# Linear attention and a feed-forward layer: queries spread evenly ahead of the wide stage, gathered in float32, half of the normalising on ScalarE

## The chip, the cores and the metric

The kernel runs on one core of a Trainium2 chip. The metric is the device time of one execution in microseconds. An execution's time is a little longer than its span in the trace, which runs from the first to the last instruction.

## What is computed

The reference is linear attention with random features, and a feed-forward layer on its result. For each of 8 batches and 8 heads (576 tokens, head dimension 64, 128 features):

```python
def phi(x):
    proj = np.einsum('bhsd,md->bhsm', x, omega)
    sq = np.sum(x * x, axis=-1, keepdims=True) / 2.0
    h = proj - sq
    h = h - np.max(h, axis=-1, keepdims=True)
    return np.exp(h) / np.sqrt(m)
q_p, k_p = (phi(q_s), phi(k_s))
kv = np.einsum('bhsm,bhsd->bhmd', k_p, v)
z = np.sum(k_p, axis=2)
num = np.einsum('bhsm,bhmd->bhsd', q_p, kv)
den = np.einsum('bhsm,bhm->bhs', q_p, z)[..., None] + 1e-06
attn_out = num / den
x = attn_out.transpose(0, 2, 1, 3).reshape(B * S, H * D)   # 4608 x 512
h = x @ w_in                                                # 512 x 2048
g = h - np.tanh(h)
out = g @ w_out                                             # 2048 x 512
```

## The kernel before

The 4608 tokens are cut into 18 chunks of 256. A pair of heads (128 rows) is called c and runs from 0 to 3, so x of a chunk has four pieces. Nearly all products are made in a one-pass float format from an operand split in two: the rounded part and the rest (`xh` and `xl` for x, `gh` and `gl` for g, `qh` and `ql` for the queries' features).

Three stages follow each other on TensorE:

- Chunks 0 and 1, taken together as tiles 512 wide, while the weights are decoded (to about 173 us).
- Chunks 2 to 5 singly, 256 wide. `ffn_h` makes the tiles h of a chunk, two blocks of the 2048 at a time (s from 0 to 7), and `ffn_out` their products with w_out.
- Chunks 6 to 17 in six pairs of 512 tokens, the wide stage. `wide_h` makes one h tile 512 wide per block f (0 to 15) and its g; `wide_out` and the "last" products follow. h has two PSUM banks, so block f=2 waits until f=0's bank has been read by the tanh and by the subtraction g = h - tanh(h).

Attention runs beside this, in generators. A key unit (b, c) makes kv and z of a batch and a pair of heads. A query unit (ch, c), `q_unit`, makes one piece of x: it loads q (`qf`, by a DMA that SP issues), splits it (`qx`), makes the features (`pj`, then the exponential in `phi`), multiplies them by z to get the denominator (`dn`, line 350), takes the reciprocal and scales its four feature tiles by it (lines 354 to 359), transposes them (`pt`, line 366), splits them (`qh`, line 384, and `ql`, line 385), multiplies by kv (`pn`, lines 391 and 392) and gathers the result in `later` (lines 396 to 399: two copies on ScalarE, two additions on VectorE). From chunk 3 on pt and pn share one PSUM bank, and so do the units after each other. `x_split` (lines 407 and 408) then makes `xh` on ScalarE and `xl` on VectorE.

Both `later` and `xh`/`xl` hold two chunks, at ch % 2. Before the change a unit of chunks 3 to 5 calls `x_split` itself right after its gather (line 402), into the place that chunk ch - 2 was read from; for pairs from 6 on `next_x` splits both chunks at once when all their units are done.

What goes first is set in two steps. Tables of numbers give the beat at which each unit's generator is started (`start`, lines 643 to 655); the main program calls `beat()` twice per s or f, and each beat advances every open generator by one step. `tick((), True)` advances them without work of the main program, where a chunk is needed and its units aren't done. The instructions so recorded are then put in order by a scheduler, engine by engine. Each engine executes its list strictly in that order.

The engine that scales a tile is taken in rotation from a list (`norm`); from chunk 3 on this list reads:

```python
norm=[nc.vector, nc.vector, nc.vector, nc.scalar]
```

## Time and profile before

| | us |
|---|---|
| median of 3 runs | 1074.54 |
| lowest and highest | 1073.91, 1076.31 |
| the profiled execution's own time | 1075.36 |
| its span in the trace | 1073.6 |
| TensorE busy | 1041.5 (97%) |
| VectorE busy | 854.3 (80%) |
| ScalarE busy | 695.0 (65%) |
| GpSimd busy | 440.9 (41%) |

PE is TensorE's matmuls, DVE is VectorE, ACT is ScalarE, POOL is GpSimd, SP issues DMAs. The shares are means over stages: VectorE's falls after 900 us, when the last queries are done. Where an instruction waited, its row ends with the idle time of its engine in brackets and with the instruction that ended it. The granted clock is a share of TensorE's 2.4 GHz; it has two levels, 1.2 and 2.4 GHz, so a value between is a mean over a stretch.

### The profile page before, as it was taken

The page shows a single profiled execution, that of the slowest core. Times are in us where ns is not written, and L with a number is a line of the kernel's source. Part 1 is how long each engine was busy: PE and PEld are TensorE (multiplying, and loading weights), DVE is VectorE, ACT ScalarE, POOL GpSimd, SP SyncE. Part 2 cuts the span into 40 slices and gives each one's busy share as a digit, 9 for nine tenths or more (in the row PEclk, how much of TensorE's full clock was granted, in tenths as well). Part 3 has the DMA queues.
Part 4 walks back from the last instruction along what each step waited for, and adds up shares of the span by engine and source line. Part 5 has one row for each costly group of instructions (what it writes and reads, how often), then busy time and mean ns, then how long its engine had stood idle before and what let it go on. Part 6 is the DMA issues. An engine that isn't in the chain of part 4 may idle for free.

```text
span 1073.6 us, 19114 instructions
## 1 busy us (share of the span) xinstructions
PE 1041.5 (97%) x5608; PEld 889.1 (83%) x5608; DVE 854.3 (80%) x3006; ACT 695.0 (65%) x1809; POOL 440.9 (41%) x745
## 2 busy tenths in 40 slices
PE   8988999999999899899999999999999999999998
PEld 7766888999988898688888888888887888888886
DVE  5999995999999989989989888899889958742220
ACT  5997655777777778677767676677666746532220
POOL 3634540544543322556545563656355402221320
PEclk8999999999999999899999999999999999999999
DMA  8952722111211101222234332443243314332301
GB/s 261 295 172 90 283 96 70 33 34 53 55 53 33 53 16 57 72 77 78 78 109 137 103 118 88 130 138 117 65 142 115 104 45 146 114 101 82 104 1 39
DMA packets 85960, 106.18 MB, mean 99 GB/s; under 512 B 17632, under 2 KB 67936, under 8 KB 83808
## 3 DMA queue, kind: packets, MB, share of 16 engines
q1 hardware_dynamic: 85776, 104.92, 31.1%
q8 instruction: 45, 0.74, 0.3%
q14 instruction: 59, 0.48, 0.1%
q10 hardware_dynamic: 80, 0.03, 0.0%
HBM read 87.10 MB, written 17.83 MB: 98 GB/s over the span
## 4 chain that ended last, share of the span: by engine, by line
PE 67%; DVE 22%; issue 5%; ACT 4%; POOL 1%; DMA 0%; DVEq 0%; POOLq 0%; ACTq 0%
PE h_w L532 19%; PE h L471 7%; PE last L545 4%; PE last L547 4%; PE last L546 4%; DVE junk L350 3%; PE po_w L547 3%; PE po_w L546 3%; PE po_w L545 3%; PE po L489 2%; PE po L490 2%; PE po L491 2%; PE pk L269 2%; PE pt L366 2%; DVE phi_q L359 2%
## 5 line engine op out<-in xcount | busy, mean ns | idle before, releaser
L532 PE MATMUL h_w<-xh,w 128*128 128x512 f32 x768 | 253.9, 394 | 2.7 <-DVE g_w L536 2.6
L532 PEld LDWEIGHTS h_w<-xh,w 128*128 128x128 f32 x768 | 144.1, 189 | 31.1 <-DVE g_w L536 4.2
L532 PE MATMUL h_w<-xl,w 128*128 128x512 f32 x384 | 151.3, 394 | 0.9 <-DVE xl L408 0.9
L471 PE MATMUL h<-xh,w 128*128 128x256 f32 (+1 forms) x640 | 147.2, 307 | 3.8 <-DVE g L476 2.2
L540 POOL CAST w<-g_w 128x256 fp32r<-128x256 f32 x96 | 41.0, 427 | 224.2 <-DVE g_w L536 208.5
L471 PEld LDWEIGHTS h<-xh,w 128*128 128x128 f32 x640 | 107.5, 190 | 11.8 <-DVE g L476 3.1
L350 DVE CUSTOM_DVE_ANT_0 junk<-phi_q,zb 128x128 f32<-128x128 f32 (+1 forms) x320 | 105.3, 331 | 13.1 <-ACT phi_q L153 1.0
L536 DVE TENSOR_TENSOR g_w<-h_w,g_w 128x512 f32<-128x512 f32 x96 | 66.0, 687 | 60.6 <-ACT g_w L535 59.9
L471 PE MATMUL h<-xl,w 128*128 128x256 f32 (+1 forms) x320 | 97.5, 305 | 2.1 <-DVE xl L408 2.1
L153 ACT ACTIVATE phi_q<-phi_q,nb_q 128x128 f32<-128x128 f32 x240 | 82.5, 394 | 19.6 <-DVE nb_q L149 18.7
L535 ACT ACTIVATE g_w<-h_w 128x512 f32<-128x512 f32 x96 | 56.8, 591 | 57.1 <-PE h_w L532 53.4
L253 POOL TENSOR_TENSOR khl<-phi_ka,khl 128x256 fp32r<-128x256 f32 x48 | 38.3, 798 | 127.3 <-DVE khl L252 105.5
L532 PEld LDWEIGHTS h_w<-xl,w 128*128 128x128 f32 x384 | 72.8, 190 | 14.4 <-DVE xl L408 1.3
L541 POOL TENSOR_TENSOR w<-g_w,w 128x256 fp32r<-128x256 f32 x96 | 80.0, 833 | 4.6
L440 POOL TENSOR_SCALAR a<-a 128x1024 f32<-128x1024 f32 x14 | 59.0, 4213 | 54.4 <-ACT a L436 36.0
L545 PE MATMUL po_w<-w,ge_w 128*128 128x512 f32 x192 | 75.9, 395 | 0.0
L545 PE MATMUL last<-w 128*128 128x512 f32 x192 | 75.4, 393 | 0.0
L546 PE MATMUL po_w<-w,ge_w 128*128 128x512 f32 x192 | 75.3, 392 | 0.0
L547 PE MATMUL last<-w 128*128 128x512 f32 x192 | 75.2, 392 | 0.0
L546 PE MATMUL last<-w 128*128 128x512 f32 x192 | 75.1, 391 | 0.0
L537 ACT CAST ge_w<-g_w 128x256 fp32r<-128x256 f32 x96 | 39.1, 407 | 55.6 <-DVE g_w L536 53.9
L547 PE MATMUL po_w<-w,ge_w 128*128 128x512 f32 x192 | 72.2, 395 | 1.3 <-DVE ge_w L538 1.2
(173 smaller groups left out, 2911.9 us busy)
## 6 DMA issues: line engine op xcount, KB each, us to landing
w<-w_in SPq DMA_DIRECT2D x320, 128.0 KB, 2.4
raw<-w SPq DMA_DIRECT2D x16, 1024.0 KB, 8.1
kf<-kT SPq DMA_DIRECT2D x32, 288.0 KB, 3.2
qf<-qT SPq DMA_DIRECT2D x72, 128.0 KB, 2.2
out<-o SPq DMA_DIRECT2D x36, 256.0 KB, 2.1
w_in<-w SPq DMA_DIRECT2D x16, 512.0 KB, 3.4
v<-vt SPq DMA_DIRECT2D x24, 288.0 KB, 2.9
v<-va SPq DMA_DIRECT2D x8, 288.0 KB, 5.9
```

The lines of the kernel that those rows point to most:

```text
L153: nc.scalar.activation(ph[:, j], ph[:, j], AF.Exp, bias=nb[:, j : j + 1], scale=-1.0)
L350: nc.vector.tensor_tensor_reduce(bank("junk")[r], ph[r, i], kvs[b, c][1][r, h], scale=1.0, scalar=EPS, op0=ALU.mult, op1=ALU.add, accum_ou ...
L440: engine.tensor_scalar(a.bitcast(F32), a.bitcast(F32), 2.0**-15, 122879.9921875, op0=ALU.max, op1=ALU.min)
L471: nc.tensor.matmul(o, w_, x, start=i == 0, stop=i == len(prods) - 1)
L532: nc.tensor.matmul(p, w_, x, start=i == 0, stop=i == len(prods) - 1)
L535: nc.scalar.activation(g, p, AF.Tanh)
L536: nc.vector.tensor_sub(g, p, g)
L540: nc.gpsimd.tensor_copy(hi, g[:, 1])
L541: nc.gpsimd.tensor_sub(lo, g[:, 1], hi.bitcast(F32))
L545: nc.tensor.matmul(o, h, wt[f][:, 0, DM:], start=f == 0, stop=False)
L546: nc.tensor.matmul(o, h, wt[f][:, 1, DM:], start=False, stop=False)
L547: nc.tensor.matmul(o, l, wt[f][:, 0, DM:], start=False, stop=f == NF - 1)
```

## The change

A query unit of chunks 3 to 5 no longer splits its x. It gathers x in float32 in `later`, once the chunk that holds the place (ch - 2) has been split (the set `split`). The main program splits a chunk: `x_of(ch)` makes the four pieces' `xh` and `xl`, at the chunk's start if it hasn't been done, or ahead of that, in the chunk before, if all four units have been recorded by then. Chunks 6 and 7 are split in the same way during chunk 5 where they can be; later pairs as before. The tables of starts are new for the queries of chunks 3 to 9 and the keys of batches 2 to 4. The rotation of the scaling is `[nc.vector, nc.scalar]`, so two of four tiles go to each engine.

```diff
--- before.py
+++ after.py
@@ -390,16 +390,13 @@
                 w = kvs[b, c][0][:, h * P : (h + 1) * P]
                 nc.tensor.matmul(pn[:, h, s:e], w, qh[:, h, s:e], start=True, stop=False)
                 nc.tensor.matmul(pn[:, h, s:e], w, ql[:, h, s:e], start=False, stop=True)
-        while ch >= C0 and gathered < (ch - C0) // 2:
+        while ch > 3 and ch - 2 not in split:
             yield
         xs = later[:, c, ch % 2 * TC : ch % 2 * TC + TC]
         nc.scalar.copy(xs[0:D], pn[D:P, 0])
         nc.scalar.copy(xs[D:P], pn[0:D, 1])
         nc.vector.tensor_add(xs[0:D], pn[0:D, 0], xs[0:D])
         nc.vector.tensor_add(xs[D:P], pn[D:P, 1], xs[D:P])
-        if ch < C0:
-            yield
-            x_split(ch, c, xs, nc.vector)
         xdone[ch] = xdone.get(ch, 0) + 1
 
     def x_split(ch, c, x, engine):
@@ -556,7 +553,7 @@
 
     need = {b: (b * S) // TC for b in range(B)}
     xdone = {}
-    gathered = 0
+    split = {2}
     gens = []
 
     def tick(new=(), force=False):
@@ -627,7 +624,7 @@
     kvf.clear()
     ak = open_pool("ak")
     mode.update(
-        chain=False, native=False, norm=[nc.vector, nc.vector, nc.vector, nc.scalar], junk=[junk],
+        chain=False, native=False, norm=[nc.vector, nc.scalar], junk=[junk],
         hi=nc.scalar, pj=["pj0"], pk=["pk"], pt=["pj0"],
         phi=(ak, 3), qh=(ak, 1), ql=(ak, 1), kf=(ak, 1), kx=(ak, 1), qf=(ak, 1),
         qx=(ak, 1), vr=(ak, 1), khl=(ak, 2), vhl=(ak, 2), zs=(ak, 1), c1=(ak, 1), kvs=(ak, 1))
@@ -644,14 +641,14 @@
         a, j = (ch - C0) // 2, (ch - C0) % 2 * NC
         for c in range(NC):
             if ch < C0 + 2:
-                k = [(28,32,36,40),(41,45,49,53),(56,60,63,66),(58,68,72,75),(78,81,83,85)][ch - 3][c]
+                k = [(28,31,34,37),(43,46,49,52),(40,55,58,63),(61,66,69,72),(75,78,80,83)][ch - 3][c]
             else:
-                k = begins(a - 1) + -9 + 10 * (j + c) // 2
+                k = begins(a - 1) + (-4 + 9 * (j + c) // 2 if a == 1 else -9 + 5 * (j + c))
             start.setdefault(k, []).append(("q", ch, c))
     for b in range(2, B):
         a = ((b * S) // TC - C0) // 2
         for c in range(NC):
-            k = [31,51][b - 2] + [5,5][b - 2] * c if b < 2 + len([31,51]) else begins(a - 1) + -18 + 11 * c
+            k = [28,48,82][b - 2] + [5,5,9][b - 2] * c if b < 2 + len([28,48,82]) else begins(a - 1) + -18 + 11 * c
             start.setdefault(k, []).append(("k", b, c))
     t = 32 - 2 * (NF - done)
     assert min(start) >= t and all(k == int(k) for k in start)
@@ -669,12 +666,24 @@
     ffn_store(0)
     mode.update(pj=["pj0", "pj1"], pt=["pt"])
     prev = None
+
+    def x_of(ch):
+        split.add(ch)
+        for c in range(NC):
+            x_split(ch, c, later[:, c, ch % 2 * TC : ch % 2 * TC + TC], nc.vector)
+
     for ch in range(2, C0):
         out_tiles(ch)
+        while xdone[ch] < NC:
+            tick((), True)
+        if ch not in split:
+            x_of(ch)
         for s in range(NS):
-            while ch > 2 and xdone.get(ch, 0) < NC:
-                tick((), True)
+            if s > 0 and ch + 1 not in split and xdone.get(ch + 1) == NC:
+                x_of(ch + 1)
             g = (ch, s, *ffn_h(ch, s))
+            if ch == C0 - 1 and s == NS - 1 and xdone.get(C0 + 1) == NC:
+                x_of(C0 + 1)
             beat()
             if prev is not None:
                 ffn_out(*prev)
@@ -690,13 +699,17 @@
     mode.update(o=["g", "gl"])
 
     def next_x(a):
-        nonlocal gathered
-        for ch in (C0 + 2 * a, C0 + 2 * a + 1):
+        pair = (C0 + 2 * a, C0 + 2 * a + 1)
+        for ch in pair:
             while xdone.get(ch, 0) < NC:
                 tick((), True)
-        gathered = a + 1
-        for c in range(NC):
-            x_split(slice(0, 2), c, later[:, c].rearrange("p (j t) -> p j t", j=2), nc.vector)
+        if split.isdisjoint(pair):
+            for c in range(NC):
+                x_split(slice(0, 2), c, later[:, c].rearrange("p (j t) -> p j t", j=2), nc.vector)
+            split.update(pair)
+        for ch in pair:
+            if ch not in split:
+                x_of(ch)
 
     next_x(0)
     for a in range(NL):
```

What the new tables and the new place of the split do to the order stands in the programs. The names carry chunk and c: `qf_5_0` is the load of unit (5,0), `pt_7_3` the transposes of unit (7,3), `ka4_1`, `km4_1` and `kb4_1` the parts of key unit (4,1); `h_4_0` is the h tile of chunk 4, s=0, `h_w0_1` that of the first wide pair, f=1.

SP, the loads of queries, keys (`kf`) and values (`v`) from the one of (4,0) on, before:

```order
L84 DMA qf_4_0_2331<-qT 128x256
L84 DMA kf_2_3_2691<-kT 128x576
L84 DMA qf_4_1_2624<-qT 128x256
L235 DMA v_2_2_2335<-vt 128x576
L84 DMA qf_4_2_2895<-qT 128x256
L84 DMA kf_3_0_3029<-kT 128x576
L502 DMA out<-o_640_2867 128x512
L235 DMA v_2_3_2693<-vt 128x576
L502 DMA out<-o_512_2864 128x512
L84 DMA qf_4_3_3141<-qT 128x256
L84 DMA qf_5_0_3334<-qT 128x256
```

With the change, the same place:

```order
L84 DMA qf_5_0_2414<-qT 128x256
L84 DMA kf_2_3_2591<-kT 128x576
L235 DMA v_2_2_2256<-vt 128x576
L84 DMA qf_4_0_2589<-qT 128x256
L84 DMA qf_4_1_2821<-qT 128x256
L84 DMA kf_3_0_2948<-kT 128x576
L499 DMA out<-o_640_2967 128x512
L235 DMA v_2_3_2593<-vt 128x576
L499 DMA out<-o_512_2964 128x512
L84 DMA qf_4_2_3008<-qT 128x256
L84 DMA qf_4_3_3226<-qT 128x256
```

The load of unit (5,0), which stood behind all of chunk 4, now stands ahead of (4,0).

TensorE, where chunk 4 begins. Before, the last products of unit (4,3) and the first of chunk 4:

```order
L392 MATMUL pn_4_3_3512<-ql_4_3_3437,kvw_2_3_3235 128x128
L391 MATMUL pn_4_3_3512<-qh_4_3_3436,kvw_1_3_996 128x128
L145 MATMUL pj_ka3_1_2_3478<-om_89,kx_3_1_3377 128x256 x2
L392 MATMUL pn_4_3_3512<-ql_4_3_3437,kvw_1_3_996 128x128
L391 MATMUL pn_4_3_3512<-qh_4_3_3436,kvw_2_3_3235 128x128
L392 MATMUL pn_4_3_3512<-ql_4_3_3437,kvw_2_3_3235 128x128
L489 MATMUL po1_3_2780<-w13_1523,gh_3_6_3571 128x512
L490 MATMUL po1_3_2780<-w13_1523,gh_3_6_3571 128x512
L491 MATMUL po1_3_2780<-w13_1523,gl_3_6_3572 128x512
L471 MATMUL h_4_0_3832<-xh_100,w0_220 128x256
```

With the change, from the transposes of unit (4,3) on:

```order
L366 MATMUL pt_4_3_3503<-ident_64,phi_q4_3_3320 128x128 x4
L145 MATMUL pj_km3_1_0_3514<-om_89,kx_3_1_3348 128x256
L468 MATMUL h_4_0_3945<-xh_100,w0_220 128x256
L468 MATMUL h_4_1_4099<-xh_100,w2_448 128x256
L145 MATMUL pj_q5_1_0_3525<-om_89,qx_5_1_3474 128x256 x2
L305 MATMUL pk_3_0_3059<-ident_64,c1_3_0_3456 128x128 x2
L307 MATMUL pk_3_0_3059<-zhl_3_0_3453,ones_92 128x256 x2
L468 MATMUL h_4_0_3945<-xl_101,w0_220 128x256
L468 MATMUL h_4_0_3945<-xh_100,w0_220 128x256
L468 MATMUL h_4_1_4099<-xl_101,w2_448 128x256
L468 MATMUL h_4_1_4099<-xh_100,w2_448 128x256
L391 MATMUL pn_4_3_3583<-qh_4_3_3508,kvw_1_3_996 128x128
```

Before, the last unit's products were all ahead of chunk 4's first tile; now they stand inside its first two tiles, which wait for c=3 behind them.

TensorE, where the wide stage begins. Before, from the products that follow unit (7,2) to the first of (7,3):

```order
L145 MATMUL pj_km4_1_0_5498<-om_89,kx_4_1_5375 128x256
L145 MATMUL pj_q8_1_0_5556<-om_89,qx_8_1_5507 128x256 x2
L269 MATMUL pk_4_1_5401<-khl_4_1_0_5462,vhl_4_1_0_5463 128x256 x2
L366 MATMUL pt_7_3_5366<-ident_64,phi_q7_3_5205 128x128 x4
L532 MATMUL h_w0_0_5642<-xh_100,w0_220 128x512
L532 MATMUL h_w0_1_5705<-xh_100,w1_337 128x512
L269 MATMUL pk_4_1_5401<-khl_4_1_2_5468,vhl_4_1_2_5469 128x256 x2
L532 MATMUL h_w0_0_5642<-xl_101,w0_220 128x512
L532 MATMUL h_w0_0_5642<-xh_100,w0_220 128x512
L532 MATMUL h_w0_1_5705<-xl_101,w1_337 128x512
L532 MATMUL h_w0_1_5705<-xh_100,w1_337 128x512
L391 MATMUL pn_7_3_5392<-qh_7_3_5371,kvw_3_3_4577 128x256
```

With the change:

```order
L145 MATMUL pj_ka4_1_0_5424<-om_89,kx_4_1_5401 128x256 x2
L145 MATMUL pj_ka4_1_2_5430<-om_89,kx_4_1_5401 128x256 x2
L269 MATMUL pk_4_0_5037<-khl_4_0_5_5278,vhl_4_0_5_5279 128x256 x2
L366 MATMUL pt_7_3_5252<-ident_64,phi_q7_3_5098 128x128 x4
L529 MATMUL h_w0_0_5571<-xh_100,w0_220 128x512
L529 MATMUL h_w0_1_5638<-xh_100,w1_337 128x512
L529 MATMUL h_w0_0_5571<-xl_101,w0_220 128x512
L529 MATMUL h_w0_0_5571<-xh_100,w0_220 128x512
L529 MATMUL h_w0_1_5638<-xl_101,w1_337 128x512
L529 MATMUL h_w0_1_5638<-xh_100,w1_337 128x512
L269 MATMUL pk_4_0_5037<-khl_4_0_7_5284,vhl_4_0_7_5285 128x256 x2
L391 MATMUL pn_7_3_5290<-qh_7_3_5257,kvw_3_3_4508 128x256
```

The parts of key unit (4,1) and of query unit (8,1) that stood ahead of the transposes of (7,3) have made way for earlier parts of the key units, and (8,1) is gone from here; the rows from the transposes to `pn_7_3` are the same in kind.

## Rows read from the trace of the kernel before

**Rows 1.** The page, part 1: busy us (share of the span) xinstructions of the engines.

```profile
PE 1041.5 (97%) x5608; PEld 889.1 (83%) x5608; DVE 854.3 (80%) x3006; ACT 695.0 (65%) x1809; POOL 440.9 (41%) x745
```

**Rows 2.** Busy time by stretch; the columns are named in the first row.

```profile
core 0: us, PE busy (x) PEld busy (x) DVE busy (x) ACT busy (x) POOL busy (x), PEclk, DMA share, GB/s
245.00:300.00 55.00, 54.77 (x365) 49.49 (x364) 51.48 (x201) 42.45 (x116) 24.64 (x47) 1.00 0.19 53
300.00:353.00 53.00, 51.07 (x352) 46.56 (x350) 48.52 (x193) 39.21 (x108) 22.01 (x42) 1.00 0.14 43
353.00:416.00 63.00, 60.30 (x413) 55.39 (x412) 57.01 (x243) 47.94 (x128) 19.90 (x39) 1.00 0.14 41
416.00:445.00 29.00, 22.79 (x108) 17.54 (x107) 26.98 (x108) 23.69 (x64) 6.83 (x15) 0.93 0.23 71
445.00:548.00 103.00, 103.00 (x531) 87.19 (x530) 92.52 (x349) 70.38 (x197) 57.04 (x109) 0.99 0.24 70
600.00:640.00 40.00, 39.02 (x202) 31.97 (x201) 35.67 (x132) 29.14 (x78) 24.52 (x45) 1.00 0.34 108
815.00:840.00 25.00, 23.36 (x117) 18.08 (x116) 22.68 (x95) 16.13 (x46) 12.88 (x25) 1.00 0.37 113
```

**Rows 3.** The chain that ended last, in order of time: start us, us, what.

```profile
240.11 3.23 PE h L471 x27
...
365.70 2.73 DMA v<-vt
...
1004.05 2.72 PE h_w L532 x12
```

**Rows 4.** TensorE in order of time: start us, us, line, op, idle before <-releaser.

```profile
167.96 0.40 PE L145 MATMUL pj_q<-om,qx 128*128 128x256 f32 x2
...
367.18 0.39 PE L471 MATMUL h<-xl,w 128*128 128x256 f32 x1 [2.13 <-DVE xl L408]
...
421.48 0.60 PE L366 MATMUL pt<-ident,phi_q 128*128 128x128 f32 x4
...
430.01 0.71 PE L366 MATMUL pt<-ident,phi_q 128*128 128x128 f32 x4
...
436.50 0.63 PE L366 MATMUL pt<-ident,phi_q 128*128 128x128 f32 x4 [1.10 <-DVE later L399]
...
438.91 0.50 PE L532 MATMUL h_w<-xl,w 128*128 128x512 f32 x1 [0.89 <-DVE xl L408]
...
443.27 0.50 PE L532 MATMUL h_w<-xh,w 128*128 128x512 f32 x1 [1.94 <-DVE g_w L536]
```

**Rows 5.** Instructions on pt and later: min/median/max ns, first and last start.

```profile
L384 ACT CAST qh<-pt x60: 560/586/607, 186.1 to 969.4; 128x512 fp32r<-128x512 f32 x60
L385 DVE TENSOR_TENSOR ql<-pt,qh x60: 674/685/694, 186.7 to 970.0; 128x512 fp32r<-128x512 f32 x60
...
L396 ACT COPY later<-pn x60: 368/369/372, 192.5 to 975.7; 64x256 f32<-64x256 f32 x60
L397 ACT COPY later<-pn x60: 363/364/368, 192.9 to 976.1; 64x256 f32<-64x256 f32 x60
L398 DVE TENSOR_TENSOR later<-pn,later x60: 385/411/418, 193.4 to 976.5; 64x256 f32<-64x256 f32 x60
L399 DVE TENSOR_TENSOR later<-pn,later x60: 427/428/429, 193.9 to 976.9; 64x256 f32<-64x256 f32 x60
```

**Rows 6.** Lines 359 and 357, the scaling: ns min/median/max; and three in sequence.

```profile
L359 DVE TENSOR_SCALAR phi_q<-phi_q,dn x204: 270/281/1056, 34.2 to 939.9; 128x128 f32<-128x128 f32 x102
...
L357 ACT ACTIVATE phi_q<-phi_q,dn x84: 386/402/599, 32.2 to 938.8; 128x128 f32<-128x128 f32 x84
...
427.11 0.08 DVE L149 DVE_READ_ACCUMULATOR2_ANT nb_ka<- 128x1 f32 x1
```

**Rows 7.** VectorE from 107 to 443 us by shape: busy us, mean ns, idle before.

```profile
L408 DVE TENSOR_TENSOR xl<-later,xh 128x256 fp32r<-128x256 f32 x16 | 6.9, 432 | 1.9 <-ACT xh L407 1.7
...
L408 DVE TENSOR_TENSOR xl<-later,xh 128x512 fp32r<-128x512 f32 x4 | 2.8, 688 | 0.1
```

## The prediction

> **What bounds the kernel now.** The page's first line comes first: TensorE is busy 97% of the span [rows 1], and its work isn't changed. So the question is where it stands still, and I read that from stretches, not from the page's shares. The table of stretches [rows 2] shows TensorE full from 445 to 548, but idle for 0.23, 1.93, 2.70 and 6.21 us in the four stretches from 245 to 445. VectorE is busy there for 51.48 of 55, 48.52 of 53, 57.01 of 63 and 26.98 of 29 us (94, 92, 90 and 93%), ScalarE for 77, 74, 76 and 82%. So VectorE is the fullest of the engines that TensorE waits for, directly or at second hand.
>
> Idle time understates it: a matmul of 512 columns is shown as 0.39 us long, but in a dense run twelve take 2.72 us, so 0.227 us each, and one of 256 takes 3.23/27 = 0.120 us [rows 3]; a pause under 0.16 us never shows. So I count starts. Unit (3,0) has its first projection at 167.96, and the wide stage its first product of f=2 at 443.27 [rows 4]: 275.3 us. The order has 456 matmuls of 512 columns between, 1,116 of 256, 134 of 128 (0.11 us each: four transposes in 0.60 us, the last one's modelled end included) and 32 narrower ones (about 0.1): 103.5 + 133.9 + 14.7 + 3 = 255 us. **20 us are lost there**: that is the pot.
>
> Half of it lies at the end. From the transposes of unit (7,2) at 421.48 to 443.27 [rows 4] are 21.8 us; the order has 26, 35 and 12 matmuls of the three sizes there, 5.9 + 4.2 + 1.3 = 11.4 us. So **10.4 us go at the change from chunk 5 to the wide stage**, of which 3.3 between the transposes of (7,2) and (7,3), 4.5 until c=3 of x has been split (438.91), and 2.5 until the first wide tile's PSUM bank is free (443.27). The granted clock is 0.93 over these 29 us [rows 2]; after the pause it stood at 1.2 GHz for a while, which the same numbers contain.
>
> Why it takes that long is in the unit itself. pt and pn of every unit share one bank, so units go through it in single file: qh 0.59, ql 0.69, two copies 0.37 and 0.36, two additions 0.41 and 0.43 [rows 5], with 0.3 to 0.5 us for each of the two groups of four on TensorE: 3.7 us, and some 4.5 us with the handovers. Between the transposes of (7,2) and (7,3) 8.5 us passed: the rest is VectorE's queue. The transposes of (8,0) stood 1.10 us for an addition of the same kind [rows 4].
>
> **The change, part by part.** *Half of the normalising to ScalarE.* All 60 later units have three scalings on VectorE and one on ScalarE; now two and two. On VectorE one lasts 0.281 us, three behind each other 0.67, so 0.20 to 0.28 us each; on ScalarE it is 0.402 [rows 6]. VectorE loses 60 x 0.20 to 0.28 = 12 to 17 us in all, and 4 to 5.6 us in the 20 units of chunks 3 to 7; ScalarE gains 24 us, 8 of them there. Row for row the same scaling is dearer on ScalarE by 0.12 to 0.20 us. I still count it as a gain, since VectorE is the fuller engine by 11 to 18 points in each of the four stretches [rows 2], and ScalarE's added 8 us over these 200 us raise it by four. What hides ScalarE's part is its own idle fifth; where that is gone, each costs 0.40 us ahead of a tanh. I put 0.5 us (0 to 2) for that.
> The Trainium skill, "ScalarE: Activation LUTs", Rules for kernel authors, says to use VectorE and not ScalarE for a mul, as up to about 3 times faster per element in bf16. These fp32 rows show a factor of 1.4. By the rule this edit alone would cost time, 60 x 0.12 to 0.20 = 7 to 12 us if it were on the path, in place of a gain; that is the third rival below.
>
> *Chunks 3 to 5 gathered in float32, split later.* Before, a unit split its x itself, so chunk 5's couldn't run until chunk 3's tiles had been read. Now x stays in `later`, and unit (5,0) goes as early as (4,0) did, as the order shows. The same copies and subtractions are made. For chunks 6 and 7 eight pieces of 0.432 us take the place of four of 0.688 [rows 7], 0.7 us more on VectorE, but six of them well ahead: nothing. Each unit takes its one qf load along on SP; that buffer is single in both kernels, so the load waits for the unit ahead as before: nothing, if the units are spread.
>
> *The new starts.* They thin out what stands before the wide stage: chunk 7 from beat 75 and not 78, keys of batch 4 from 82 and not 78, chunk 8 from 92 and not 87. So VectorE has less to do in chunk 5, and more in chunks 3 and 4.
>
> Now the sum, by place.
> 1. Change to the wide stage. The order leaves 18, 33 and 14 matmuls from the transposes of (7,2) to f=2, 4.1 + 4.0 + 1.5 = 9.6 us. (7,2) to (7,3) has 3.0 us of work in it, and takes 4.5 us when VectorE is free, 8.5 as now: I take 6.3, nearer to the first, since (7,2) and (7,3) project much earlier than before; 3.3 lost. From there to the split of c=3 the unit's 4.5 us and the split's 0.4 + 0.4 stand against 4.3 us of work; now 8.9 us: I take 7.3, 3.0 lost. Then the first tile's tanh and subtraction against 2.3 us of work: 1.2 lost. Together 7.5 (2.5 to 12) for 10.4: **-2.9**.
> 2. The other 10 us of the pot. The largest single piece is at 367.18, 2.13 us of waiting for the split of chunk 5's last unit [rows 4], which sat on VectorE behind a v load that landed late [rows 3]. Now chunk 5's last pn stands 5 us of TensorE's work ahead of chunk 5, where it stood inside its first products, and VectorE has 4 to 5.6 us less to do. I take 4 of 10 as left (1 to 8): **-6**.
> 3. What is late next: chunk 4. Its last unit now comes inside chunk 4's first products. From its transposes to f-pair 2 the order has 57 matmuls of 256 and 14 of 128 columns, 8.4 us. Unit and split need 5.3 us, then come 3.2 us of products behind c=3 and a tanh and subtraction: 10 us at the least, 13 as at the wide stage now. It costs 1.5 to 6; I take **+3.5**, as VectorE's queue is long there.
> 4. ScalarE ahead of the tanh: **+0.5**.
> 5. Wide passes: 40 units, so 8 to 11 us less on VectorE over 540 us. TensorE stands still 0.98 us in 600 to 640 and 1.64 in 815 to 840, where VectorE is at 89 and 91% [rows 2]. I take **-1.5** (-4 to +2).
> 6. Chunk 9 comes later; the order leaves 5 us between its last pn and the first product that needs it: **+0.4** (0 to 2).
>
> The sum is -6.0 us. The profiled execution took 1075.36 us, 0.82 above the median of 1074.54; so 1069.4 there, and **1068.5 us** against the median.
>
> **The rivals.**
> - *The wide stage's wait all but goes.* If VectorE's queue is empty there, the loss falls to its lower bound, 2.5 us for 7.5, the pot's rest to 1 for 4, and the clock never falls: 8 us more, 1060.5. For it: VectorE's load in chunk 5 falls most. Against: one bank for pt and pn, which the change leaves. 0.17.
> - *The wait only moves.* Chunk 4 pays what the wide stage pays now, 10 us for 3.5: 1075. For it: the same chain, the same bank, a VectorE that is fuller there than before. Against: chunk 4's units follow each other at a longer distance than (7,2) and (7,3). 0.16.
> - *ScalarE becomes the bound* and the kernel is slower. Every added scaling stands in a strict queue ahead of a tanh, an evacuation or a copy of x. Where ScalarE's share in a stretch reaches VectorE's, 0.40 us in replaces 0.20 to 0.28 out: 20 x 0.16 = 3 us in chunks 3 to 7, the gains of 1 and 2 are gone, and chunk 4 costs its 3.5: about 1081. For it: 82% in the last stretch. Against: 74 to 77% in the three before. 0.11. The Trainium skill's rule above would have it so.
> - That the scalings don't move can be excluded: the order shows two on each engine.
>
> **How the numbers follow.** The forecast itself, 2.2 to 10 us faster, has 0.56. About 0.2% (2.1 us) is what a measurement can tell from none. Faster: 0.56 + 0.17 = 0.73; the wait that only moves gives the same, 0.16; slower 0.11. The range takes in the first rival and the second: 1060.5 to 1075.5.
>
> **What would show it.** Right: 120 scalings on ScalarE instead of 60 in the later units; the first dense wide products 5 to 12 us earlier than 443.27; chunk 5 without a wait for xl; a wait for xl of some us at the start of chunk 4; VectorE under 85% in chunk 5. Wrong: ScalarE named as releaser of wide or chunk products, VectorE still over 90% in the last 30 us before the wide stage, or a low clock at chunk 4.

## The result, and the profile after

| | us |
|---|---|
| median after (12 runs) | 1078.22 |
| lowest and highest | 1077.17, 1079.84 |
| median of the kernel before, beside it (12 runs) | 1074.72 |
| ratio, 95% interval | 1.0031 [1.0023, 1.0040] |
| span in the trace, after (before 1073.6) | 1076.4 |

The change makes the kernel 3.5 us slower, where 6.0 us faster was forecast; the time lies above the range.

The first part of the page, and busy time by stretch (columns as in [rows 2]):

```profile
PE 1044.1 (97%) x5608; PEld 887.7 (82%) x5608; DVE 846.2 (79%) x2950; ACT 713.0 (66%) x1873; POOL 441.8 (41%) x745
```

```profile
245.00:300.00 55.00, 54.41 (x366) 49.69 (x367) 50.86 (x200) 43.03 (x121) 25.51 (x48) 1.00 0.18 53
300.00:316.00 16.00, 13.25 (x88) 11.97 (x89) 15.22 (x57) 12.83 (x37) 8.91 (x19) 0.89 0.18 46
...
306.00:309.00 3.00, 2.82 (x11) 2.47 (x12) 2.88 (x16) 2.95 (x9) 0.32 (x1) 0.50 0.17 44
...
316.00:366.00 50.00, 48.91 (x327) 44.42 (x326) 46.95 (x189) 38.50 (x108) 19.07 (x37) 1.00 0.15 44
366.00:416.00 50.00, 49.78 (x340) 45.83 (x340) 43.29 (x186) 37.68 (x104) 7.95 (x15) 1.00 0.09 29
416.00:441.00 25.00, 21.64 (x107) 16.78 (x107) 19.69 (x74) 19.12 (x52) 10.21 (x20) 0.93 0.20 65
441.00:550.00 109.00, 106.71 (x533) 86.49 (x533) 95.66 (x357) 76.94 (x215) 58.36 (x104) 1.00 0.25 75
```

Against [rows 1], VectorE is 8.1 us less busy and ScalarE 18.0 us more. Against [rows 2], the wide stage's start is relieved: VectorE is busy 79% from 416 to 441, where it was 93%. There are two new places. From 300 to 316 TensorE idles 2.75 us, and for 3 us the granted clock is 0.50, the level of 1.2 GHz. And the first wide pass, where TensorE was full, idles 2.29 us.

The first place is chunk 4. TensorE there:

```profile
298.80 0.60 PE L366 MATMUL pt<-ident,phi_q 128*128 128x128 f32 x4
...
301.27 0.33 PE L391 MATMUL pn<-qh,kvw 128*128 128x128 f32 x1 [0.19 <-DVE ql L385]
...
303.43 0.71 PE L269 MATMUL pk<-khl,vhl 128*128 128x256 f32 x4 [0.26 <-POOL khl L253]
305.87 0.70 PE L145 MATMUL pj_kb<-om,kx 128*128 128x256 f32 x2 [1.74 <-DVE vhl L262]
...
308.26 0.56 PE L468 MATMUL h<-xl,w 128*128 128x256 f32 x1
...
312.92 0.39 PE L468 MATMUL h<-xh,w 128*128 128x256 f32 x1 [0.35 <-DVE g L473]
```

VectorE, from the last addition of unit (4,3) to its `xl`:

```profile
304.76 0.43 DVE L399 TENSOR_TENSOR later<-pn,later 64x256 f32<-64x256 f32 x1
...
305.89 0.42 DVE L132 TENSOR_TENSOR qx<-qf,qx 64x256 fp32r<-64x256 f32 x1
306.34 0.22 DVE L262 TENSOR_TENSOR vhl<-v,vhl 64x64 fp32r<-64x64 f32 x1
306.59 0.42 DVE L133 TENSOR_TENSOR qx<-qf,qx 64x256 fp32r<-64x256 f32 x1
...
307.67 0.51 DVE L405 TENSOR_TENSOR xl<-later,xh 128x256 fp32r<-128x256 f32 x1
```

and ScalarE:

```profile
305.44 0.37 ACT L146 COPY phi_kb<-pj_kb 128x256 f32<-128x256 f32 x1
305.84 0.41 ACT L404 CAST xh<-later 128x256 fp32r<-128x256 f32 x1
```

Unit (4,3) takes 9.5 us from its transposes (298.80) to its first product with `xl` (308.26). Its gather ends at 305.19; `xh` follows on ScalarE, behind a copy, to 306.25, and `xl` only at 307.67, since VectorE does other units' work in between. TensorE's longest stop there, 1.74 us, is put down to VectorE too (`vhl`), and after it the clock is down.

The wide stage's start did what was forecast:

```profile
423.98 0.60 PE L366 MATMUL pt<-ident,phi_q 128*128 128x128 f32 x4
...
429.00 0.63 PE L366 MATMUL pt<-ident,phi_q 128*128 128x128 f32 x4 [0.39 <-DVE later L399]
431.30 0.38 PE L391 MATMUL pn<-qh,kvw 128*128 128x256 f32 x1
...
435.57 0.47 PE L145 MATMUL pj_km<-om,kx 128*128 128x256 f32 x1 [2.02 <-ACT kvs L310]
...
440.81 0.50 PE L529 MATMUL h_w<-xh,w 128*128 128x512 f32 x1
```

From (7,2)'s transposes to f=2 it takes 16.8 us where it took 21.8 [rows 4], and (7,3) follows (7,2) after 5.0 us, not 8.5. The longest stop that is left, 2.02 us, is for a key unit's copy `kvs` on ScalarE, which is full just then, and the granted clock is low behind it:

```profile
433.00:436.00 3.00, 0.98 (x6) 0.59 (x6) 2.61 (x13) 2.89 (x10) 2.55 (x5) 0.94 0.00 0
436.00:441.00 5.00, 5.00 (x22) 3.78 (x22) 4.87 (x25) 4.85 (x16) 1.57 (x6) 0.69 0.36 99
```

Chunk 5's first products (from 361.71 on) no longer wait for `xl`, 2.13 us before; the one stop among the first 24 is for an earlier tile's g:

```profile
365.01 0.39 PE L468 MATMUL h<-xh,w 128*128 128x256 f32 x1 [0.82 <-DVE g L473]
```

The second place, the first wide pass (441 to 559), by waits (engine, line waited for: us in all, times, longest):

```profile
PEld po_w L544 <- DVE ge_w L535: 1.4, 2, 0.9
...
PEld pk L269 <- POOL zt L274: 1.1, 2, 0.9
PEld last L542 <- DVE g_w L533: 1.1, 1, 1.1
PEld po_w L542 <- ACT ge_w L534: 0.6, 2, 0.4
...
PE last L542 <- DVE g_w L533: 0.7, 1, 0.7
```

It is no single wait: TensorE stops for VectorE, GpSimd and ScalarE by turns, 1.1 us at the longest. Nor is it the granted clock, which is 1.00 over this pass in after and 0.98 in before.

**Where the time went.** Idle time understates it, so I count as the prediction did: the time from each matmul's start to the next one's, less the lower quartile of that spacing for its kind in the kernel before; what is above is lost. By this the pot of 20 us is 24.6. The prediction had 0.11 us for 128 columns, with a modelled end in it; four transposes in a dense run take 0.35 us (298.80 to 299.15). The marks are the first projection of (3,0), the first product of chunk 4's block s=2, and the first of f=2 in each wide pass. From (3,0) on TensorE executes the same 4,856 matmuls in both kernels, as many of each width, so losses can be compared even where work moves across a mark. How finely kinds are told apart shifts whole columns of the tables by up to 3 us, and a difference between two kernels by under 1 us.

| lost, us | (3,0) to chunk 4 | to the wide stage | first wide pass | next three passes |
|---|---|---|---|---|
| before | 4.0 | 20.6 | 3.5 | 12.9 |
| after | 11.5 | 13.3 | 8.7 | 11.7 |
| difference | +7.5 | -7.3 | +5.2 | -1.2 |

What the wide stage's start gained, chunk 4 (and 2.0 us of the 7.5 already in chunk 3, between 220 and 250) paid back. The first wide pass comes on top. The span's +2.8 us also holds -1.2 us ahead of (3,0)'s projection (166.73 for 167.96). That is no effect of the change: up to there the four compute engines have the same instructions in the same order in all 20 kernels of this document, and the mark lies anywhere from 165.40 to 167.96.

The stretches themselves in the page's terms, before:

```profile
167.96:305.77 137.81, 137.58 (x928) 126.15 (x927) 120.56 (x474) 102.86 (x276) 59.71 (x111) 1.00 0.14 43
305.77:443.27 137.50, 126.66 (x814) 112.31 (x813) 125.96 (x518) 105.23 (x283) 42.43 (x81) 0.99 0.16 48
```

and after:

```profile
166.73:312.92 146.19, 141.42 (x935) 128.49 (x934) 126.30 (x490) 110.58 (x299) 61.50 (x116) 0.99 0.15 44
312.92:440.81 127.89, 123.22 (x793) 109.93 (x793) 112.73 (x454) 98.14 (x270) 38.96 (x74) 0.99 0.14 43
```

VectorE is busy 7.5 us less over both, as 246.5 fell to 239.0, and still TensorE loses as much as before (24.6 and 24.8).

### The profile page after: what moved, and what is told of

Its sections match the earlier page's. It is cut to its first block, busy times and chain, and to the rows that moved or that the text cites. A ratio compares the mean times of both kernels' runs of the same rounds, so it can differ in the third digit from the quotient of the medians.

```text
span 1076.4 us, 19106 instructions
## 1 busy us (share of the span) xinstructions
PE 1044.1 (97%) x5608; PEld 887.7 (82%) x5608; DVE 846.2 (79%) x2950; ACT 713.0 (66%) x1873; POOL 441.8 (41%) x745
## 4 chain that ended last, share of the span: by engine, by line
PE 60%; DVE 26%; ACT 8%; issue 4%; POOL 1%; DMA 1%; DVEq 0%; ACTq 0%; POOLq 0%
PE h_w L529 16%; PE h L468 8%; DVE junk L350 4%; PE last L544 4%; PE last L543 4%; PE last L542 4%; PE po_w L544 3%; PE po_w L542 3%; PE po_w L543 3%; PE po L486 2%; PE po L487 2%; PE po L488 2%; DVE vhl L262 2%; DVE g_w L533 2%; PE pj_q L145 2%
## 5 line engine op out<-in xcount | busy, mean ns | idle before, releaser
L468 PEld LDWEIGHTS h<-xh,w 128*128 128x128 f32 x640 | 108.0, 191 | 14.1 <-DVE g L473 5.2
L153 ACT ACTIVATE phi_q<-phi_q,nb_q 128x128 f32<-128x128 f32 x240 | 82.5, 395 | 25.2 <-DVE nb_q L149 23.9
L529 PEld LDWEIGHTS h_w<-xl,w 128*128 128x128 f32 x384 | 72.4, 188 | 13.7 <-DVE xl L405 0.8
L357 ACT ACTIVATE phi_q<-phi_q,dn 128x128 f32<-128x128 f32 x144 | 51.3, 408 | 48.0 <-DVE dn L353 47.4
```

The lines of the kernel that those rows point to most:

```text
L153: nc.scalar.activation(ph[:, j], ph[:, j], AF.Exp, bias=nb[:, j : j + 1], scale=-1.0)
L357: e.mul(ph[:, i], ph[:, i], dn[:, i : i + 1])
L468: nc.tensor.matmul(o, w_, x, start=i == 0, stop=i == len(prods) - 1)
L529: nc.tensor.matmul(p, w_, x, start=i == 0, stop=i == len(prods) - 1)
```

## The experiments

All 18 are in the table at the end of this section, with the losses counted as above from one profiled execution each. Differences of time between kernels are taken from their ratios to the kernel before, which ran beside each. *Starts* are the tables of beats; *1 of 4* and *2 of 4* is how many of a unit's scalings go to ScalarE. Of an edit's lines only the parts that change are shown; three dots stand for lines left out.

**The parts undone, and the rotation alone.** The theories: chunk 4 pays (late units); scalings on ScalarE cost the wide pass; the late chunks 8 and 9 cost it.

`a_norm3to1`: after, with the old rotation.

```diff
-        norm=[nc.vector, nc.scalar]
+        norm=[nc.vector, nc.vector, nc.vector, nc.scalar]
```

> The changed kernel with the old rotation of the scaling, three of four tiles on VectorE. Marks are first products: of unit (3,0), of block 2 of chunk 4, of block f=2 of the first and second wide pair. In the kernel before, 137.8 us lie from (3,0) to chunk 4, 137.5 from there to the wide stage, 111.6 through the first wide pass; in the changed one 146.2, 127.9 and 118.2. Theory S (ScalarE's added scalings stand ahead of the tanh and of the rest of g, and cost the first wide pass its 6.6 us): the pass falls back to 111 to 114 us, the time to 1071 to 1074. Theory L (the later starts of chunks 8 and 9 and of the keys of batch 4 press that work into the pass): the pass stays at 117 to 120, the time at 1077 to 1083, as VectorE gets 12 to 17 us back.

Measured 1.0034 [1.0021, 1.0047], no better than after: the first pass gets back 4.0 us (4.7 lost), chunk 4 loses 3.4 more (14.9). The pass is as theory S had it (113.7 us), the time as theory L had it.

`a_late_old`: after, with the old starts of chunks 8 and 9 and of batch 4's keys.

```diff
-                k = begins(a - 1) + (-4 + 9 * (j + c) // 2 if a == 1 else -9 + 5 * (j + c))
+                k = begins(a - 1) + -9 + 10 * (j + c) // 2
...
-[28,48,82]  [5,5,9]
+[28,48]  [5,5]
```

> The changed kernel with the old starts of chunks 8 and 9 and of the keys of batch 4 (from beat 87 and 78). Theory L: the first wide pass falls back to 111 to 114 us, and what stood after the beginning of the wide stage stands ahead of it again, so the stretch from chunk 4 to the wide stage grows from 127.9 by 2 to 5 us; the time is 1073 to 1077. Theory S: the pass stays at 117 to 120 us and the time at 1078 to 1083.

1.0090 [1.0075, 1.0105]. The first pass gets back 2.4 us, but chunk 4 loses 1.9 more, the wide stage's start 3.6 and the later passes 2.5. In this pair the late starts are worth 6.3 us; with the old starts of chunks 3 to 7 (`e_late_only`, below) it is 1.7.

`b_norm1to1`: the kernel before with the new rotation.

```diff
-        norm=[nc.vector, nc.vector, nc.vector, nc.scalar]
+        norm=[nc.vector, nc.scalar]
```

> The kernel before with the new rotation of the scaling alone, two of four tiles on ScalarE. Theory S: its first wide pass grows from 111.6 to 115 or more, the time is 1077 to 1081. Theory L: the pass stays at 111 to 113 us; VectorE is relieved, so the two stretches ahead of the wide stage lose 1 to 4 us, and the time is 1070 to 1074.

1.0055 [1.0040, 1.0070]: alone, the rotation comes out 5.9 us slower, 1.8 ahead of the wide stage and 3.9 in the passes.

`a_starts_old`: after with all the old starts, so the gather, the split and the rotation.

```diff
-(28,31,34,37),(43,46,49,52),(40,55,58,63),(61,66,69,72),(75,78,80,83)
+(28,32,36,40),(41,45,49,53),(56,60,63,66),(58,68,72,75),(78,81,83,85)
...
-begins(a - 1) + (-4 + 9 * (j + c) // 2 if a == 1 else -9 + 5 * (j + c))
+begins(a - 1) + -9 + 10 * (j + c) // 2
...
-[28,48,82]  [5,5,9]
+[31,51]  [5,5]
```

> The changed kernel with all the old starts: gathering in float32, the split by the main program and the new rotation stay. If chunk 4's wait of 8 us comes from the table, that puts chunk 5's first unit ahead of chunk 4's, the stretch from (3,0) to chunk 4 falls from 146.2 to 137 to 140 us. If it comes from the split by the main program it stays above 143. Theory L: first wide pass 111 to 114; theory S: 117 to 120. The time is 1072 to 1077 by the table theory with L, 1080 and more by the split theory with S.

1.0026 [1.0016, 1.0036]. Chunk 4's stretch falls from 11.5 us lost to 4.8: that loss is the table's. But the wide stage's start loses 19.2 again.

**Do the parts add up?** `c_split_only` is `a_starts_old` with the old rotation, so the gather and split alone.

```diff
-        norm=[nc.vector, nc.scalar]
+        norm=[nc.vector, nc.vector, nc.vector, nc.scalar]
```

> The kernel after with the old starts and the old rotation (three scalings on VectorE, one on ScalarE): only the float32 gather and the separate split are left of the change. Parts add up (rotation alone cost 5.8 us, rotation with gather and split cost 2.6): 3.2 us faster than before, 0.997, with the gain ahead of the wide stage or in the passes. Parts don't add up (each new order scatters by some us): anywhere within 0.998 to 1.004, without a gain.

1.0041 [1.0027, 1.0054], 4.4 us slower instead of 3.2 faster. Parts that cost 5.9 and 4.4 us alone cost 2.8 together: prices that add up don't do that.

`c_switch`: `a_starts_old`, 2 of 4 ahead of the wide stage, 1 of 4 in it.

```diff
-    mode.update(o=["g", "gl"])
+    mode.update(o=["g", "gl"], norm=[nc.vector, nc.vector, nc.vector, nc.scalar])
```

> The kernel after with the old starts; two scalings of four on ScalarE up to chunk 5's end, one of four from the wide stage on. If the scalings on ScalarE help ahead of the wide stage, where VectorE is the fuller engine, and cost in the wide passes: up to the first wide product as the run with all old starts (441.3), passes as before (111.6 and 337.1 us where that run had 113.6 and 338.4), so 2 to 3 us faster than before, 0.9975. If their cost isn't tied to the wide passes: within 1.000 to 1.003.

1.0013 [1.0005, 1.0022], 1.4 us better than 2 of 4 throughout, but still slower than before.

`c_phase`: before with its one scaling on ScalarE put first, the same counts.

```diff
-        norm=[nc.vector, nc.vector, nc.vector, nc.scalar]
+        norm=[nc.scalar, nc.vector, nc.vector, nc.vector]
```

> The kernel before with the one scaling on ScalarE put first of the four and not last: the same counts on each engine. If the cost of the new rotation is work moved to ScalarE: no change, 0.999 to 1.001. If any other order of the instructions moves the time by some us: off by 0.3% or more to either side.

0.9989 [0.9981, 0.9998]. The total hardly moves, which by itself speaks for the counts and not for the order, but stretches do: the third wide pass loses 4.6 us instead of 1.5, the stretch to the wide stage 18.5 instead of 20.6.

`c_allv`: before with none on ScalarE.

```diff
-        norm=[nc.vector, nc.vector, nc.vector, nc.scalar]
+        norm=[nc.vector]
```

> The kernel before with all four scalings of the later units on VectorE, so 60 less on ScalarE. Theory that a scaling on ScalarE costs what stands behind it there (5.8 us for 60): some 3 to 6 us faster, 0.995 to 0.997, above all in the wide passes. Theory that VectorE is the bound (60 x 0.20 to 0.28 us more on it, 12 to 17 us in all, 4 to 6 of it ahead of the wide stage): 4 to 10 us slower, 1.004 to 1.009, above all ahead of the wide stage. Both hold, each in its stage: ahead of the wide stage 3 to 6 us longer, passes 1 to 4 us shorter.

1.0064 [1.0051, 1.0077]. Ahead of the wide stage VectorE's added work costs 3.4 us, as that theory had it. But the passes lose 3.4 more too, where fewer scalings on ScalarE should have gained: 60 more on it (`b_norm1to1`) and 60 fewer both cost there.

**Chunk 4.** In `d_50late` unit (5,0), which stands ahead of (4,0) in the single file, starts at beat 53.

```diff
-(43,46,49,52),(40,55,58,63)
+(43,46,49,52),(53,55,58,63)
```

> The kernel after with unit (5,0) started at beat 53 and not 40, behind chunk 4's units and not ahead of them. Theory that the wait at chunk 4 comes from (5,0) standing ahead of chunk 4 in the single file: the stretch from (3,0)'s projection to chunk 4's third block shrinks from 146.2 towards before's 137.8, to 138 to 142 us, and the whole to some 1072 to 1075. Rival, that the keys of batch 3 and the later chunk 4 starts fill VectorE there: it stays at 145 us or more. Either way chunk 5 may get a wait of 1 to 3 us.

1.0013 [1.0004, 1.0023]: 8.3 us lost for 11.5, though the stretch behind loses 2.3 more. From 290 to 320 the loss falls by 4 us, so (5,0) ahead of chunk 4 was most of chunk 4's wait. It was not what chunk 3 loses: from 220 to 250 the loss grows from 3.4 to 5.0 us, and TensorE's wait for chunk 3's last `xl` with it, in after:

```profile
239.75 0.39 PE L468 MATMUL h<-xl,w 128*128 128x256 f32 x1 [0.56 <-DVE xl L405]
```

and in `d_50late`:

```profile
241.35 0.39 PE L468 MATMUL h<-xl,w 128*128 128x256 f32 x1 [1.27 <-DVE xl L405]
```

From the wide stage's f=2 on, TensorE's list is the same as after's, row for row in names and widths. The first pass, which follows on another order, takes 1.7 us less; the next three take the same time to 0.1 us each. **The same order takes the same time.**

`d_4early`: that, and chunk 4 earlier.

```diff
-(43,46,49,52),(40,55,58,63)
+(40,44,47,50),(53,55,58,63)
```

> As the run with (5,0) late, and chunk 4's units started 2 to 3 beats earlier as well, so that the order has chunk 4's last unit 30 matmuls ahead of chunk 4: no wait at chunk 4, 137 to 139 us for that stretch and not 146.2, with the wide stage's gain kept (128 to 130): 1070 to 1073. If VectorE is merely full there, the time comes back as small pauses: 141 us or more, or more than 132 behind it.

0.9994 [0.9985, 1.0003]. TensorE at chunk 4, from (4,3)'s transposes on:

```profile
286.95 0.60 PE L366 MATMUL pt<-ident,phi_q 128*128 128x128 f32 x4
...
291.89 0.23 PE L391 MATMUL pn<-qh,kvw 128*128 128x128 f32 x1
...
301.88 0.39 PE L468 MATMUL h<-xl,w 128*128 128x256 f32 x1 [0.36 <-DVE xl L405]
```

The unit is 12 us earlier and the wait is 0.36 us. Yet 8.9 us are lost up to chunk 4, in small stops from 220 on, and 17.6 behind it: together 26.5, no less than before's 24.6. I had expected the stretch's length back at 137 to 139 us; it was 146.8, of which 3.2 is work that stands behind the mark in after (12 matmuls of 512 columns and 4 of 128). And the first wide pass loses 3.4 us, as before the change, with after's rotation and its late chunks 8 and 9 untouched.

`d_switch` (from after) and `d_both` (from `d_4early`), with 1 of 4 from the wide stage on, by the edit of `c_switch`:

> The kernel after with the old rotation from the wide stage on (two of four scalings on ScalarE before it, one of four in it). Chunk 4 and the wide stage's start are as after (146.2 and 127.9 us). If it is the scalings on ScalarE together with the late chunks 8 and 9 that cost the first wide pass: 113.5 us there and not 118.2, about 1074. If the late starts alone do it: 117 to 118.5, 1078.

> Both repairs in one: chunk 4's units early, (5,0) late, and the old rotation from the wide stage on. If the two costs are separate they add up: 137 to 139, 128 to 130 and 113 to 114 us for the three stretches, and 1066 to 1069 in all, faster than both kernels. If each new order scatters: 1071 to 1075.

1.0104 [1.0089, 1.0119] and 1.0007 [0.9997, 1.0017]. The same edit of the rotation costs 7.8 us in one and 1.4 in the other. In `d_switch` the first pass improves by 2.2 us, and the next three lose 20.0 for 11.7.

**Price or order?** What is left is whether the first pass's 5 us have any cause among the parts. `e_phase` is after with as many scalings on ScalarE, but of the other tiles.

```diff
-        norm=[nc.vector, nc.scalar]
+        norm=[nc.scalar, nc.vector]
```

> The kernel after with the rotation begun on ScalarE and not on VectorE: the same 120 scalings on ScalarE, but of the other tiles. If the first wide pass's 118.2 us are a price of ScalarE's scalings with the late starts: 117 to 119 again, and 1076 to 1080 in all. If they come from the order that was found: 111 to 116 there, and each other stretch off by up to 3 us to either side.

1.0001 [0.9992, 1.0010], 3.2 us faster than after. The first pass loses 3.9 us, not 8.7. Chunk 4 stays bad, with 15.0 us, and here TensorE is shown waiting for `xl`:

```profile
306.71 0.76 PE L145 MATMUL pj_q<-om,qx 128*128 128x256 f32 x2 [2.42 <-DVE nb_kb L149]
...
310.53 0.58 PE L468 MATMUL h<-xl,w 128*128 128x256 f32 x1 [1.61 <-DVE xl L405]
```

`e_late_only`: the old starts of chunks 3 to 7 and of the keys of batches 2 and 3; only chunks 8 and 9 and batch 4's keys are later. `e_late_3to1` and `e_late_phase` are the same with 1 of 4, ScalarE last or first.

```diff
-(28,31,34,37),(43,46,49,52),(40,55,58,63),(61,66,69,72),(75,78,80,83)
+(28,32,36,40),(41,45,49,53),(56,60,63,66),(58,68,72,75),(78,81,83,85)
...
-[28,48,82]
+[31,51,82]
```

> The kernel after with the old starts of chunks 3 to 7 and of the keys of batches 2 and 3; later are only chunks 8 and 9 and the keys of batch 4. Up to chunk 5 the order is that of the run with all old starts: 139.0 us to chunk 4's third block. Theory that the late starts alone make the gain ahead of the wide stage: 129 to 132 us from there to the wide stage and not 135.7; some 1071 to 1074. Rival, that the gain came from chunk 7 being earlier: 134 to 137, 1076 to 1078.

> As the run before with one scaling of four on ScalarE, so the old kernel with the new gather and split and the late starts. With the gain of the late starts and without the rotation: 138 us, then 130 to 133, then 111 to 114; 1070 to 1075. If the rotation is needed for the gain, as the run with gather and split alone suggests (1079.8 with one of four, 1077.0 with two): 1076 to 1080.

> As the run before with the one scaling on ScalarE put first: the same counts on each engine. If a rotation has a price by itself, within 1 us of that run; if the order decides, off by 2 us or more to either side. With the old code this phase was 0.8 us faster than before.

1.0010 [1.0000, 1.0019], 1.0043 [1.0026, 1.0060] and 0.9974 [0.9964, 0.9984]. With 2 of 4 the late starts gain 1.7 us and not 3 to 6; with 1 of 4 the two phases are 7.4 us apart at equal counts, and the second beats both kernels, by 2.8 and 6.1 us. Its one trace shows little of the 2.8: from (3,0)'s projection to the end it takes 905.3 us against before's 905.6, and the rest lies ahead of that mark (165.64 for 167.96), where the instructions are the same. Where that lead comes from stays open. The third wide pass of `e_late_3to1`:

```profile
672.98:788.44 115.46, 113.79 (x594) 95.64 (x593) 102.45 (x393) 82.10 (x225) 62.24 (x114) 1.00 0.38 113
```

and of `e_late_phase`:

```profile
668.98:780.44 111.46, 111.46 (x590) 95.31 (x589) 98.75 (x377) 79.30 (x218) 59.64 (x112) 1.00 0.38 117
```

One idles 1.67 us there, the other never, with 0.3 to 4% less work on each engine.

`f_late_phase1` and `f_4early_phase`: the twins of `e_late_only` and `d_4early`, with the edit of `e_phase`.

> The gather and split and the late starts of chunks 8 and 9 alone, two scalings of four on ScalarE, ScalarE first. If the order decides: off from its twin's 1076.0 by 2 us or more to either side, with no wait at chunk 4 (137 to 140 us up to its third block). If counts decide: 1075 to 1077.

> Chunk 4's units early, (5,0) late, two of four on ScalarE, ScalarE first. The order has chunk 4's last unit 3 matmuls behind the chunk's first product, and not 30 ahead of it as its twin: a wait of 1 to 4 us there, 1 to 4 us more than the twin up to chunk 4's third block. In all, if counts decide, 1074 to 1078; if the order of the later stretches decides, off from the twin's 1074.8 by more than that wait.

1.0008 [0.9999, 1.0018] and 1.0001 [0.9991, 1.0011]: within 0.8 us of their twins, as counts would have it. So a new order need not change the sum. Inside it does: `f_4early_phase` loses 5.4 in the first pass and 9.1 in the next three, its twin 3.4 and 11.2. The wait of 1 to 4 us that was expected in it at chunk 4's start was 0.26 us.

Five edits change the phase alone. They move the time by 1.2, 3.2, 7.4, 0.2 and 0.8 us (`c_phase`, `e_phase`, `e_late_phase`, `f_late_phase1`, `f_4early_phase`); only the second and third lie clearly outside of what their expectations gave to counts. The passes say more. Where two kernels' TensorE lists are the same through one of the passes 2 to 4 (row for row in names and widths), they take the same time there to within 0.5 us, whatever differs ahead: in the second 115.97 and 115.93 (`a_late_old`, `b_norm1to1`), in the third 111.25 three times and 111.30 (after, `d_50late`, `d_4early`, `e_late_only`), in the fourth 108.58, 108.51 and 108.54 (`a_norm3to1`, `c_split_only`, `e_late_3to1`). Where the lists differ, the third pass ranges from 111.1 to 115.9 us and the fourth from 107.3 to 112.2, with 1 of 4 and with 2 of 4 alike. In the first pass the same list took 118.2 and 116.5 us (after, `d_50late`), so there what comes in from ahead counts too.

| kernel | median us | ratio to before | lost to chunk 4 | to the wide stage | first pass | next three |
|---|---|---|---|---|---|---|
| before, 1 of 4 | 1074.72 | | 4.0 | 20.6 | 3.5 | 12.9 |
| after, 2 of 4 | 1078.22 | 1.0031 | 11.5 | 13.3 | 8.7 | 11.7 |
| a_norm3to1, 1 | 1077.85 | 1.0034 | 14.9 | 13.7 | 4.7 | 12.5 |
| a_late_old, 2 | 1083.93 | 1.0090 | 13.4 | 16.9 | 6.3 | 14.2 |
| b_norm1to1, 2 | 1080.25 | 1.0055 | 4.8 | 21.6 | 6.2 | 14.1 |
| a_starts_old, 2 | 1077.04 | 1.0026 | 4.8 | 19.2 | 5.3 | 14.8 |
| c_split_only, 1 | 1079.76 | 1.0041 | 4.1 | 20.6 | 5.7 | 16.3 |
| c_switch, 2 then 1 | 1076.43 | 1.0013 | 4.7 | 19.6 | 4.2 | 14.0 |
| c_phase, 1 | 1073.67 | 0.9989 | 3.6 | 18.5 | 2.5 | 15.4 |
| c_allv, 0 | 1082.13 | 1.0064 | 8.1 | 19.9 | 5.3 | 14.5 |
| d_50late, 2 | 1076.28 | 1.0013 | 8.3 | 15.6 | 7.0 | 11.7 |
| d_switch, 2 then 1 | 1086.80 | 1.0104 | 12.2 | 14.5 | 6.5 | 20.0 |
| d_4early, 2 | 1074.78 | 0.9994 | 8.9 | 17.6 | 3.4 | 11.2 |
| d_both, 2 then 1 | 1075.56 | 1.0007 | 8.9 | 17.6 | 2.9 | 12.3 |
| e_phase, 2 | 1074.68 | 1.0001 | 15.0 | 11.8 | 3.9 | 10.5 |
| e_late_only, 2 | 1075.96 | 1.0010 | 4.9 | 18.3 | 5.8 | 13.6 |
| e_late_3to1, 1 | 1079.89 | 1.0043 | 4.1 | 21.6 | 5.4 | 15.7 |
| e_late_phase, 1 | 1072.06 | 0.9974 | 3.5 | 19.0 | 9.5 | 8.8 |
| f_late_phase1, 2 | 1076.15 | 1.0008 | 4.8 | 17.2 | 5.9 | 14.2 |
| f_4early_phase, 2 | 1075.30 | 1.0001 | 9.1 | 18.4 | 5.4 | 9.1 |

The sum of the losses gives each kernel's distance from before to within 1.3 us, but for `e_late_phase`, where the losses are 0.2 us fewer and the time is 2.8 us shorter.

## Why the prediction was wrong

The forecast was -6.0 us, and the losses grew by 4.2. Of the 10.2 us between, 4.6 lie in steps 4 to 6, nearly all in the wide passes, 4.0 in step 3, 1.9 in step 2 and -0.3 in step 1.

**Step 1, the change to the wide stage: right.** 7.5 us were forecast as lost there; with the prediction's 9.6 us of work in 16.8 it was 7.2. The sum is better than its terms: (7,3) came after 5.0 us and not 6.3, and from there to f=2 it took 11.8 and not 10.8, with the 2.02 us behind ScalarE's queue, which no term had.

**Step 2, the rest of the pot: two thirds right.** Of the 20.6 lost to the wide stage in before, 10.2 lay ahead of its change (20.6 less 10.4); now 6.1 (13.3 less 7.2). That is -4.1 and not -6. Chunk 5's wait for `xl`, 2.13 us [rows 4], went as told, though VectorE was still at 94 and 87% in the two stretches around it.

**Step 3, chunk 4: the mechanism right, the term too small.** From 290 to 320 TensorE loses 6.9 us for 1.4, so +5.5 where +3.5 (1.5 to 6) was taken. Missed was that chunk 3 pays as well: 2.0 us more from 220 to 250. All nine kernels with the new starts of chunks 3 to 7 lose 3.3 to 5.0 us there, the others 0.8 to 2.5, so it comes with that table, but not with (5,0), as `d_50late` shows; which of its other starts does it wasn't tried. Together +7.5; (5,0) late gave 3.2 of it back, chunk 4 early the wait itself.

So steps 1 to 3, -5.4 in the forecast, came to +0.2. The second rival ("the wait only moves") comes nearest to what happened ahead of the wide stage, and the table says more: over the two stretches together, every one of the 20 kernels loses 22 to 30 us, 22.0 to 26.4 with the old starts of chunks 3 to 7 and some scalings on ScalarE, 23.9 to 30.3 with the new ones, mended or not. Spreading units moved the loss and didn't shrink it (24.0 us on average with the old starts, `c_allv` left out, 26.8 with the new).

**Step 4, ScalarE ahead of tanh, and step 5, the wide passes: here the mechanism failed.** For the passes it had -1.5, with a bound of +2, and no term for the first. The next three gave -1.2; the first cost +5.2. The step took the passes as a matter of engine loads. The loads moved much as forecast:

before

```profile
L359 DVE TENSOR_SCALAR phi_q<-phi_q,dn 128x128 f32<-128x128 f32 x204 | 58.4, 341 | 1.0
L357 ACT ACTIVATE phi_q<-phi_q,dn 128x128 f32<-128x128 f32 x84 | 33.2, 420 | 39.9 <-DVE dn L353 39.7
```

after

```profile
L357 ACT ACTIVATE phi_q<-phi_q,dn 128x128 f32<-128x128 f32 x144 | 51.3, 408 | 48.0 <-DVE dn L353 47.4
L359 DVE TENSOR_SCALAR phi_q<-phi_q,dn 128x128 f32<-128x128 f32 x144 | 44.6, 354 | 1.2
```

13.8 us are off VectorE (12 to 17 forecast) and 18.1 on ScalarE (24 forecast, and 144 x 0.408 less 84 x 0.420 is 23.5; neighbours overlap, so the busy time grows by less). The prediction's 0.67 us for three scalings behind each other is this row of before, not the last one of [rows 6]:

```profile
427.11 0.67 DVE L359 TENSOR_SCALAR phi_q<-phi_q,dn 128x128 f32<-128x128 f32 x3
```

But what TensorE loses in the four passes doesn't follow from it: 15.2 to 26.5 us in nine kernels with 1 of 4 (mean 19.2), 14.4 to 20.5 in ten with 2 of 4 (mean 18.3), 19.8 with none. Nearly every edit makes the scheduler write another order (18 different lists of TensorE in the first pass of the 20 kernels, 17 in the second), and the order is worth several us either way: after's 8.7 us in the first pass are 3.9 with the same counts in `e_phase`, and 3.4 in `d_4early`, which leaves the passes' code and starts alone. So neither ScalarE's scalings nor the late starts have these 5 us as a price; that after drew a bad order there is bad luck. Before's order, with 16.4 in the four passes, is better than most: by these 19 kernels, which are no random sample, I estimate that to change it costs some 2.5 us on average (they lose 18.9, four of them less than before). That term was missing, and the range (1075.5 at the top) had no room for it.

**Step 6, chunk 9 later.** +0.4 cannot be told apart from the first pass's 5.2.

**The rivals.** The side that came out was the third's, but not its mechanism. Were ScalarE the bound, taking 60 scalings off it (`c_allv`) would have gained; it cost 0.64%. The Trainium skill, "ScalarE: Activation LUTs", Rules for kernel authors, says to use VectorE and not ScalarE for a mul. A time that rises with each scaling on ScalarE isn't seen in these runs: 60 more on it cost 5.9 us (`b_norm1to1`), 60 fewer 6.9 (`c_allv`), and 2 of 4 and 1 of 4 lose alike in the passes. What one scaling costs at an unchanged order wasn't tried, as the order is found anew with each edit; it stays open, as does what makes one order of a pass 4 us better than another.

**The predicted signs.** The first wide product came 2.5 us earlier, not 5 to 12; chunk 5 was without a wait for `xl`; chunk 4 had its wait and the low clock that was named as a sign of error. VectorE under 85% in chunk 5 was missed by little, with 43.29 of 50 (87%) from 366 to 416. Of the other signs of error, VectorE over 90% ahead of the wide stage stayed away (79%), and ScalarE is named as releaser of wide products for 0.6 us in the first pass.

## What to carry to other kernels

Where a scheduler writes the order, test an edit with a control that changes the order and nothing else (here the same rotation begun one tile later), in several variants: a single pair of kernels can't tell a price of 3 us from an accident of order. Read a stretch's loss together with its neighbours': a wait that is removed by starting work earlier shows up where that work now goes. And if the kernel before is the best of many tries, give any change a charge for losing its order.

## What the runs showed that was not expected

- Two kernels with equal counts on every engine have medians of 1079.89 and 1072.06 us, while two with equal TensorE order agree in three passes to 0.1 us each, and every such pair in passes 2 to 4 to 0.5 us.
- Taking 13.8 us off VectorE and spreading its work left TensorE's loss ahead of the wide stage where it was (24.6 and 24.8 us).
- The combination that does best, the new gather and split with the late starts of chunks 8 and 9 and one scaling of four first on ScalarE, loses most of all in the first wide pass (9.5 us) and least in the next three (8.8).
